# Attention, a gated feed-forward and a routed layer of eight experts: pairs of halves between the whole slots, splits issued further ahead

## The chip, the cores and the metric

The kernel runs on one core of a Trainium2 chip. The metric is the device time of one execution in microseconds. Three runs of the kernel before gave 978.3, 983.58 and 983.2, median 983.2. The engines are TensorE (PE; PEld is its weight load), VectorE (DVE), ScalarE (ACT), GpSimd (POOL) and SyncE (SP), which issues most of the transfers. Each works through its own queue in program order.

## The reference, cut to what matters

```python
scores = cap * np.tanh(scale * q @ k.T / cap)     # 4 batches, 12 heads, 448 x 64
x = softmax(scores) @ v                           # -> 1792 tokens x 768
x = (silu(x @ w_gate) * (x @ w_val)) @ w_out      # 768 -> 1536 -> 768
do_compute = x @ w_skip > 0                       # other tokens pass unchanged
e = argmax(x @ w_route, axis=1)                   # one of 8 experts per token
out = x + softmax(x @ w_route)[e] * (relu(x @ w1[e]) @ w2[e])   # 768 -> 1024 -> 768
```

## The kernel before, in words

Up to about 747 us the kernel does attention and the feed-forward layer, four batches after one another. The change touches what follows: the expert layer. Tokens are sorted by expert into **slots** of 128 rows. A whole slot holds tokens of one expert. What is left over of two experts, at most 64 tokens each, shares a slot as a **pair of halves**. Program text is laid out for four whole slots (0 to 3; slots 0 and 1 are filled from the first three batches, before the last is routed) and two pairs, here called P0 and P1 (`NWHOLE`, `NPAIRS`, `FETCHED`). More slots stand behind conditions at the end, which these inputs don't meet.

A whole slot needs its expert's w1 and w2 as eight **pieces** of 128 x 1536 numbers (768 KB). In this text piece 2.5 is the sixth piece of slot 2. `first(i)` multiplies the slot's tokens by piece i (i = 0 to 3) into a half of the hidden layer, 9 matmuls of 512 columns; after every second one ScalarE applies relu (L1066). `turn_h` transposes a half of the hidden layer on TensorE, ScalarE casts it to rounded numbers rh and VectorE forms the rest rl; `second(i)` multiplies by piece 4 + i, 12 matmuls of 384 columns; `turn_x` transposes the next slot's tokens; `finish` (L1086) weighs the result, adds the tokens and scatters the rows.

A whole slot works in rounded parts: `split_next` (L1008) rounds a loaded piece on ScalarE (wh, L1014) and subtracts on VectorE (wl, L401), and three products stand for one. A piece of a pair stays whole (`parted` is False): a pair needs sixteen pieces, two experts' eight, P0.4a and P0.4b for its ninth and tenth, takes two of them per `first` or `second`, and multiplies them in full precision, half of the rows each, without a split.

What sets the order around the change:

- `so["raw"]`: the rooms that pieces are loaded into, eight in the expert layer: three of attention's rooms (two pair_room and head_room; here R0, R1 and H) and five opened late (raw0 to raw4; here w0 to w4).
- `so["pair"]`: the pairs of buffers for a split piece's two parts, seven: three from the pool "early" (gh0 and gl0 to gh2 and gl2), two in `more`, two in the r64 pool.
- `load_next` (L996) issues the next load on SP's queue if a room is free; `coming`, `todo`, `held` (loaded, not split) and `ready` (split, or whole) are lists kept while the program is written. `used` gives buffers back.
- `piece` (L1027), called by every `first` and `second`, issues loads while there are rooms, then, in the slots behind `LATE`, at most one split, as long as fewer than `AHEAD` (5) pieces are ready.
- `LATE` (L68) is an order written out by hand for what stands between the last feed-forward unit and slot 2: slots 0 and 1 with the last routing chain among them. `choose`, `count`, `ranks`, `tiles`, `experts`, `places`, `gates`, `at` and `entries` are short VectorE chains; `listed0` and `listed1` are matmuls that make the token lists, after which VectorE writes the index row (L1327); `gather` fetches a slot's tokens by it (L952, GpSimd); `halves0`, `halves1` and `hidden0`, `hidden1` are `turn_h`, `rows1` and `rows2` are `turn_x` of slots 1 and 2; `split` is `split_next`.
- Behind `LATE`, `slot` (L1096) runs slot 2, slot 3, P0 and P1, in this order:

```python
for i in range(4):
    first(i, n)
    if i == 2:
        turn_h(0, n=n)
second(0, n)
turn_h(1, n=n)
second(1, n)
if ahead is not None:
    turn_x(ahead)
second(2, n)
second(3, n)
finish(s)
```

Of the kernel before, what the change touches and what calls it, by code (L numbers as in the profile page):

```python
# [7 lines left out]
F32 = mybir.dt.float32  # L8
F32R = mybir.dt.float32r
# [15 lines left out]
NWHOLE = 4  # L25
NPAIRS = 2
FETCHED = 2
# [7 lines left out]
AHEAD = 5  # L35
# [30 lines left out]
    chain store  # L66
""".split()
LATE = """  # L68
    choose first1 count ranks first2 hidden0 lows0 tiles first3 experts second0 hidden1 lows1 split second1 places
    split second2 rows1 gates split second3 finish0 first0 at split first1 entries split first2 listed0 halves0 split  # L70
    first3 listed1 gather gather gather gather second0 halves1 split second1 rows2 split second2 split second3 finish1
""".split()


# [1 line left out]
def tile_attn_moe_moe(  # L76
# [26 lines left out]
    PIECE = 1536  # L103
    MAXWHOLE = FETCHED + (N + (E - 1) * 63 + 127) // 128
# [30 lines left out]
    count = const.tile([T, E], F32, name="count")  # L135
    fit = const.tile([T, 6, E], F32, name="fit")
    early = const.tile([T, FETCHED], F32, name="early")
# [23 lines left out]
    def scratch(room):  # L161
        used = [0]

        def take(*shape):
            n = 1
            for d in shape:
                n *= d
            a = room[:, used[0]:used[0] + n]
            used[0] += n
            assert used[0] <= room.shape[1]  # L170
            if len(shape) == 1:
                return a
            names = " ".join("abc"[:len(shape)])
            return a.rearrange(f"p ({names}) -> p {names}", **dict(zip("abc", shape)))

        return take
# [41 lines left out]
    def gates(b):  # L218
        gt, sh = gate[:, NC * b:NC * b + NC], rt["sh"]
        nc.scalar.activation(out=sh, in_=sh, func=ACTF.Exp)  # L220
        yield V.tensor_reduce(gt, sh, axis=AX.X, op=ALU.add)
        yield V.tensor_scalar(gt, gt, EPS, None, op0=ALU.add)
        yield V.reciprocal(gt, gt)
# [148 lines left out]
    def slot_pieces(e_reg):  # L372
        a = [
            (w1[bass.ds(e_reg, 1), 128 * kk:128 * (kk + 3), 512 * half:512 * half + 512], 3)
            for half in range(F2 // 512) for kk in range(0, KD, 3)
        ]
        return a + [(w2[bass.ds(e_reg, 1), 128 * f:128 * (f + 2)], 2) for f in range(0, KF2, 2)]

    def load_piece(raw, piece):
        src, n = piece  # L380
        nc.sync.dma_start(
            out=raw.rearrange("p (k f) -> p k f", k=n), in_=src.rearrange("o (k p) f -> p (o k) f", p=128)
        )
# [3 lines left out]
    def expert(src):  # L387
        return nc.values_load(src, engines=SP, min_val=0, max_val=E - 1)

    def pieces_of(s):  # L390

        if s < FETCHED:
            return [(p, True) for p in slot_pieces(expert(early_i[0:1, s:s + 1]))]
        if s < MAXWHOLE:
            return [(p, True) for p in slot_pieces(expert(es_i[0:1, s:s + 1]))]
        o = MAXWHOLE + 2 * (s - MAXWHOLE)
        both = zip(*(slot_pieces(expert(es_i[0:1, o + i:o + i + 1])) for i in range(2)))
        return [(p, False) for ps in both for p in ps]

    def split_low(engine, low, full, high):  # L400
        engine.tensor_tensor(low, full, high.bitcast(F32), op=ALU.subtract)  # L401
# [25 lines left out]
    def whole(exact):  # L427
        with ExitStack() as ph:

            def pools(side):  # L430
                stack = ph.enter_context(ExitStack())

                def pool(name, bufs, **kw):
                    kw.setdefault("reuse_waits", "tile")
                    return stack.enter_context(tc.tile_pool(name=name, bufs=bufs, side=side, **kw))

                return stack, pool
# [466 lines left out]
            so = {"raw": [], "pair": [], "xg": [], "auto": False}  # L904

            def open_early():
                qks[0][0].close()
                right.close()
                _, pool = pools("right")
                p = pool("early", 1)  # L910
                psum = pool("ps_e", 1, space=PSUM)
                so["raw"] += [x[:, 0:PIECE] for x in pair_room + [head_room]]
                so["pair"] += [[p.tile([128, PIECE], F32R, name=f"{n}{i}") for n in ("gh", "gl")] for i in range(3)]
                so["odd"] = p.tile([128, PIECE], F32R, name="gl3")
                so["xg"] += [p.tile([128, DM], F32, name=f"xg{i}") for i in range(FETCHED)]
                so["x"] = [p.tile([128, KD, 128], F32R, name=n) for n in ("xgh", "xgl")]
                so["h"] = [[p.tile([128, KF2 // 2, 128], F32R, name=f"{n}{i}") for n in ("rh", "rl")] for i in range(2)]
                so["room"] = p.tile([128, 1024], F32, name="big_room")[0:T]
                so["row"] = p.tile([128, S], F32, name="row2")
                so["ph"] = [psum.tile([128, 512], F32, name=f"ph{i}") for i in range(2)]  # L920
                so["tp"] = [psum.tile([128, 512], F32, name=f"tp{i}") for i in range(2)]
                for xg in so["xg"]:
                    nc.gpsimd.memset(xg, 0.0)
# [62 lines left out]
            def turn_h(half, later=None, n=1):  # L986
                src = so["hid"][:, 512 * half:512 * half + 512]
                if n == 1:
                    turned(*so["h"][half], src, later)
                else:  # L990
                    turned(so["h32"][:, KF2 // 2 * half:KF2 // 2 * (half + 1)], None, src)


            coming, todo, held, ready = [], [], [], []

            def load_next():  # L996
                while so["raw"] and not todo:
                    if not coming:
                        return False
                    todo.extend(pieces_of(coming.pop(0)))  # L1000
                if not so["raw"]:
                    return False
                piece_, parted = todo.pop(0)
                held.append((so["raw"].pop(0), parted))
                load_piece(held[-1][0], piece_)
                return True

            def split_next():  # L1008
                raw, parted = held.pop(0)
                if not parted:  # L1010
                    ready.append((raw,))
                    return
                wh, wl = parts = so["pair"].pop(0)
                nc.scalar.copy(wh, raw)  # L1014
                split_low(nc.vector, wl, raw, wh)
                so["raw"].append(raw)
                ready.append(parts)
# [9 lines left out]
            def piece():  # L1027
                while load_next():
                    pass

                n = 1
                while so["auto"] and held and len(ready) < AHEAD and (not held[0][1] or n and so["pair"]):
                    n -= held[0][1]
                    split_next()
                if not ready:
                    split_next()
                return ready.pop(0)
# [75 lines left out]
            at = {load_part: 8}  # L1113
# [149 lines left out]
            for word in OPENING:  # L1263
                name = word.rstrip("0123456789")
                x = int(word[len(name):])
# [36 lines left out]
            b, last, take = B - 1, so["last"], scratch(so["late"][0:T])  # L1302

            def all_of(*chains):
                return lambda: [any(False for _ in chain()) for chain in chains]
# [13 lines left out]
            def list_(b0):  # L1319
                for b in range(b0, b0 + 2):  # L1320
                    listed(pl, rhs_[b % 2], rt["rv"][:, NC * b:NC * b + NC], b == 0, b == B - 1)
                    if b < 2:
                        put(b + 2, rhs_[b])
                if b0:
                    to = lists[:, :, FETCHED:]
                    V.tensor_tensor(to, to, pl.rearrange("p (a s) -> p a s", a=2), op=ALU.add)
                    V.tensor_copy(idx[:, FETCHED:], to[:, 0])  # L1327
# [4 lines left out]
                while load_next():  # L1332
                    pass

            order = list(range(NWHOLE)) + [MAXWHOLE + i for i in range(NPAIRS)]
            gathered = iter(order[FETCHED:])

            def next_gathered():
# [5 lines left out]
            while load_next():  # L1344
# [4 lines left out]
                "places": all_of(lambda: places(rank, take)), "at": all_of(lambda: last_at(take, room)),  # L1349
                "entries": all_of(entered), "experts": all_of(experts_known),  # L1350
                "listed0": lambda: list_(0), "listed1": lambda: list_(2),
                "gates": all_of(lambda: gates(b)), "split": split_next,
                "hidden0": lambda: turn_h(0, 0), "hidden1": lambda: turn_h(1, 1),
                "lows0": lambda: split_low(V, *lows.pop(0)), "lows1": lambda: split_low(V, *lows.pop(1)),
                "gather": next_gathered, "finish0": lambda: finish(0), "finish1": lambda: finish(1),
# [28 lines left out]
    with tc.manual_schedule():  # L1384
# [57 lines left out]
        with tc.If(big > 0) as cmp:  # L1442
            whole(True)
        with cmp.Else():
            whole(False)
# [31 lines left out]
```

## Time and profile before

| | us |
|---|---|
| median of three runs | 983.2 |
| the profiled execution | 982.64 |
| its span | 980.9 |
| PE busy in the span | 898.1 (92%) |
| DVE busy | 580.1 (59%) |
| ACT busy | 465.1 (47%) |
| POOL busy | 99.1 (10%) |

Busy shares are means over stages with different limits; the expert layer is the last quarter of the span. Times in rows count from the start of the span. [...]

### The profile page before, as it was taken

What the parts mean: (1) busy time and instruction counts of PE and PEld (TensorE: products, weight loads), DVE (VectorE), ACT (ScalarE), POOL (GpSimd) and SP (SyncE); (2) the same over time, 40 slices, a digit from 0 to 9 for tenths busy, and PEclk for the clock granted to TensorE, in tenths of its full rate; (3) what the DMA queues carried; (4) which work ended last, traced back from release to release, by engine and by line L of the source; (5) the groups of instructions that cost most, each with busy time, mean ns of one, the idle gap of its engine ahead of it and who ended that gap; (6) DMA issues with size and microseconds to landing.
All of it is one profiled execution on the core that took longest, in us unless ns stands there. A gap on an engine that the chain in (4) does not pass through costs nothing. (4 is left out here: it accounts for less than half of the span.)

```text
span 980.9 us, 12535 instructions
## 1 busy us (share of the span) xinstructions
PE 898.1 (92%) x4664; PEld 676.4 (69%) x4664; DVE 580.1 (59%) x906; ACT 465.1 (47%) x553; POOL 99.1 (10%) x66
## 2 busy tenths in 40 slices
PE   6899999999999999999999999999999775665984
PEld 2236787776788888778888888999987663544521
DVE  2768899998377666557666743565664943332000
ACT  5887667656464556446555532333342341313100
POOL 1000000000022221212221220000101020000000
PEclk9999999999999999999999999999999988667998
DMA  6996888898764344257343235453376654332894
GB/s 134 195 262 177 221 240 233 227 256 214 185 154 110 84 125 125 57 115 178 94 110 106 65 84 130 134 198 125 90 223 194 211 174 164 108 131 96 310 391 159
DMA packets 226020, 161.55 MB, mean 165 GB/s; under 512 B 158860, under 2 KB 186508, under 8 KB 225936
## 3 DMA queue, kind: packets, MB, share of 16 engines
q1 hardware_dynamic: 224048, 157.12, 57.1%
q0 software_dynamic: 960, 3.16, 0.9%
q8 instruction: 43, 0.70, 0.3%
q14 instruction: 41, 0.34, 0.1%
q10 hardware_dynamic: 928, 0.23, 0.1%
HBM read 140.01 MB, written 22.02 MB: 165 GB/s over the span
## 5 line engine op out<-in xcount | busy, mean ns | idle before, releaser
L748 PE MATMUL mo<-xhl,wh 128*128 128x448 f32 x576 | 215.1, 373 | 0.0
L750 PE MATMUL mo<-xhl,wl 128*128 128x448 f32 x576 | 210.4, 365 | 0.0
L749 PE MATMUL mo<-xhl,wh 128*128 128x448 f32 x576 | 210.3, 365 | 0.0
L401 DVE TENSOR_TENSOR wl<-raw,wh 128x768 fp32r<-128x768 f32 x108 | 117.1, 1084 | 69.8 <-ACT wh L735 69.0
L735 ACT CAST wh<-raw 128x768 fp32r<-128x768 f32 x108 | 89.9, 833 | 76.5 <-PE mo L749 49.5
L748 PEld LDWEIGHTS mo<-xhl,wh 128*128 128x128 f32 x576 | 108.1, 188 | 22.2 <-issue 11.0
L750 PEld LDWEIGHTS mo<-xhl,wl 128*128 128x128 f32 x576 | 108.2, 188 | 8.9 <-DVE wl L401 0.2
L749 PEld LDWEIGHTS mo<-xhl,wh 128*128 128x128 f32 x576 | 108.3, 188 | 7.9
L748 PE MATMUL mo<-hh,wh 128*128 128x448 f32 x288 | 108.2, 376 | 1.1 <-ACT x L795 1.1
L750 PE MATMUL mo<-hh,wl 128*128 128x448 f32 x288 | 105.3, 366 | 0.0
L749 PE MATMUL mo<-hl,wh 128*128 128x448 f32 x288 | 105.3, 366 | 0.0
L787 ACT ACTIVATE s<-mo 128x448 f32<-128x448 f32 x48 | 26.1, 544 | 110.6 <-PE mo L750 107.7
L535 ACT ACTIVATE arena<-ps,inv_sb 112x896 f32<-112x896 f32 x72 | 68.8, 1008 | 4.9 <-PE ps L525 4.9
L542 ACT ACTIVATE arena<-arena,cap_sb 112x1792 f32<-112x1792 f32 x36 | 64.6, 1793 | 1.1
L748 PEld LDWEIGHTS mo<-hh,wh 128*128 128x128 f32 x288 | 54.1, 188 | 11.8 <-issue 4.9
L570 POOL TENSOR_TENSOR sums<-arena 112x896 f32<-112x896 f32 x11 | 23.2, 2111 | 385.7 <-ACT arena L542 385.7
L750 PEld LDWEIGHTS mo<-hh,wl 128*128 128x128 f32 x288 | 54.1, 188 | 4.6
L749 PEld LDWEIGHTS mo<-hl,wh 128*128 128x128 f32 x288 | 54.1, 188 | 4.1
L581 PE MATMUL bank<-arena,arena 112*64 112x448 f32 x264 | 54.9, 548 | 1.3 <-ACT w L706 0.8
L790 DVE SCALAR_TENSOR_TENSOR s<-s,mo 128x448 f32<-128x448 f32 x48 | 29.6, 616 | 32.4 <-PE mo L750 31.5
L706 ACT ACTIVATE w<-raw 128x768 f32<-128x768 f32 x36 | 32.9, 914 | 31.3 <-DVE wl L401 13.6
L1086 DVE SCALAR_TENSOR_TENSOR o<-py,lists,xg 128x768 f32<-128x768 f32 x6 | 6.1, 1017 | 69.3 <-PE py L1050 69.3
(283 smaller groups left out, 1368.6 us busy)
## 6 DMA issues: line engine op xcount, KB each, us to landing
raw<-ws SPq DMA_DIRECT2D x54, 768.0 KB, 4.7
raw<-in_moe_w_dram SPq DMA_DIRECT2D x35, 768.0 KB, 6.4
pair_room<-in_moe_w_dram SPq DMA_DIRECT2D x20, 768.0 KB, 6.0
ws<-w SPq DMA_DIRECT2D x36, 384.0 KB, 5.8
raw<-in_moe_w_gate_dram SPq DMA_DIRECT2D x12, 768.0 KB, 5.9
raw<-in_moe_w_val_dram SPq DMA_DIRECT2D x12, 768.0 KB, 5.5
raw<-in_moe_w_out_dram SPq DMA_DIRECT2D x12, 768.0 KB, 5.1
head_room<-in_moe_w_dram SPq DMA_DIRECT2D x9, 768.0 KB, 5.9
```

Source lines behind the costliest of these rows:

```text
L401: engine.tensor_tensor(low, full, high.bitcast(F32), op=ALU.subtract)
L535: nc.scalar.activation(out=t[:, j], in_=ps[:, :, 0:S], func=ACTF.Tanh, scale=inv_sb[0:T])
L542: nc.scalar.activation(out=ts[part], in_=ts[part], func=ACTF.Exp, scale=cap_sb[0:T])
L570: nc.gpsimd.tensor_tensor(sm, ts[0][:, 0], ts[0][:, 1], op=ALU.add)
L581: nc.tensor.matmul(pv[64 * i:64 * i + 64], lhsT=hd["vn"][:, i, c], rhs=hd["t"][c // 2][:, c % 2, i], start=c == 0, stop=c == NC - 1,)
L706: nc.scalar.activation(out=w32, in_=raws[u][:, :, 1].bitcast(F32), func=ACTF.Abs)
L735: nc.scalar.copy(wh, w32s[w])
L748: nc.tensor.matmul(ps, lhsT=wh, rhs=mh, start=start, stop=False)
L749: nc.tensor.matmul(ps, lhsT=wh, rhs=ml, start=False, stop=False)
L750: nc.tensor.matmul(ps, lhsT=wl, rhs=mh, start=False, stop=stop)
L787: nc.scalar.activation(out=s, in_=cur[op], func=ACTF.Tanh, scale=0.5)
L790: nc.vector.scalar_tensor_tensor(s, in0=s, scalar=0.5, in1=cur.pop(op), op0=ALU.mult, op1=ALU.mult)
```

## The change

The slots now run in the order 0, 1, 2, P0, 3, P1. `piece` may issue two splits per call instead of one, and only split pieces count against `AHEAD`. `LATE` has more `split` words (sixteen where nine were, and their place moves: the chains places, gates, at and entries and the lists stand behind more of them); such a word does nothing if no piece is held or no pair is free. When a piece that stays whole is to be loaded, no room is free and no piece that has to be split is held, `load_next` takes one of the three early pairs that is free out of `so["pair"]` for good and adds its two buffers to `so["raw"]` as rooms. So the rooms become fourteen and the pairs four.

```diff
 LATE = """
-    choose first1 count ranks first2 hidden0 lows0 tiles first3 experts second0 hidden1 lows1 split second1 places
-    split second2 rows1 gates split second3 finish0 first0 at split first1 entries split first2 listed0 halves0 split
-    first3 listed1 gather gather gather gather second0 halves1 split second1 rows2 split second2 split second3 finish1
+    choose first1 count ranks first2 hidden0 lows0 tiles first3 experts second0 hidden1 lows1 split second1 split
+    split second2 rows1 split second3 finish0 split first0 places split gates split first1 at split first2 halves0
+    entries split split first3 split listed0 second0 halves1 split listed1 gather gather gather gather split second1
+    split rows2 split second2 split split second3 finish1 split
 """.split()
...
-                so["pair"] += [[p.tile([128, PIECE], F32R, name=f"{n}{i}") for n in ("gh", "gl")] for i in range(3)]
+                so["pair"] += [
+                    [p.tile([128, PIECE], F32R, tag=f"{n}{i}", name=f"{n}{i}") for n in ("gh", "gl")] for i in range(3)
+                ]
+
+                so["lent"], so["early"] = list(so["pair"]), p
...
             def load_next():
-                while so["raw"] and not todo:
+                if so["raw"] and not todo:
                     if not coming:
                         return False
                     todo.extend(pieces_of(coming.pop(0)))
+
+                if not so["raw"] and todo and not todo[0][1] and not any(x[1] for x in held):
+                    for i, parts in enumerate(so["lent"]):
+                        if any(parts is x for x in so["pair"]):
+                            so["pair"] = [x for x in so["pair"] if x is not parts]
+                            so["lent"][i] = None
+                            so["raw"] += [
+                                so["early"].tile([128, PIECE], F32, tag=f"{n}{i}", name=f"{n}{i}_whole") for n in ("gh", "gl")
+                            ]
+                            break
...
-                n = 1
-                while so["auto"] and held and len(ready) < AHEAD and (not held[0][1] or n and so["pair"]):
+                n = 2
+                while so["auto"] and held and (
+                    not held[0][1] or n and so["pair"] and sum(len(x) > 1 for x in ready) < AHEAD
+                ):
                     n -= held[0][1]
                     split_next()
...
+            def split_if():
+                while load_next():
+                    pass
+                if held and so["pair"]:
+                    split_next()
+
-            order = list(range(NWHOLE)) + [MAXWHOLE + i for i in range(NPAIRS)]
+            order = list(range(NWHOLE))
+            for i in range(NPAIRS):
+                order.insert(FETCHED + 1 + 2 * i, MAXWHOLE + i)
...
-                "gates": all_of(lambda: gates(b)), "split": split_next,
+                "gates": all_of(lambda: gates(b)), "split": split_if,
```

## Rows read from the trace of the kernel before

**Rows 1.** The page's strip of forty slices: TensorE's granted clock in tenths.
```profile
PEclk9999999999999999999999999999999988667998
```
**Rows 2.** Windows: stretch, length, PE, PEld, DVE, ACT, POOL busy, clock, DMA, GB/s.
```profile
811.00:861.00 50.00, 30.79 (x98) 24.70 (x98) 17.20 (x14) 14.18 (x14) 2.29 (x1) 0.73 0.41 135
861.00:913.00 52.00, 33.56 (x101) 26.27 (x103) 15.83 (x12) 11.53 (x12) 2.27 (x1) 0.67 0.38 128
913.00:937.00 24.00, 23.89 (x128) 9.28 (x124) 0.85 (x2) 3.23 (x6) 0.98 (x1) 1.00 0.89 335
937.00:971.00 34.00, 27.41 (x119) 9.63 (x118) 1.54 (x2) 2.37 (x4) 0.98 (x1) 1.00 0.87 329
```
**Rows 3.** TensorE's waits, 811 to 913: total us, times, longest; the largest.
```profile
PE py L1050 <- ACT gh L1014: 12.2, 6, 2.1
PE py L1050 <- DVE gl L401: 7.9, 6, 1.4
PE ph L1050 <- DVE gl L401: 7.4, 5, 2.5
...
```
**Rows 4.** Timeline of slot 2: start, us, engine; idle before and its releaser.
```profile
825.16 0.59 ACT L967 CAST rh<-tp 128x512 fp32r<-128x512 f32 x1 [6.01 <-PE tp L966]
825.64 1.48 ACT L1014 CAST gh<-raw 128x1536 fp32r<-128x1536 f32 x1
...
827.15 1.76 DVE L401 TENSOR_TENSOR gl<-raw,gh 128x1536 fp32r<-128x1536 f32 x1 [0.68 <-ACT gh L1014]
...
828.96 0.79 PE L1050 MATMUL ph<-gl,xgh 128*128 128x512 f32 x1 [1.29 <-DVE gl L401]
```
**Rows 5.** Windows in slot 3, TensorE's clock behind unbroken matmuls; columns as in rows 2.
```profile
866.00:869.00 3.00, 3.00 (x8) 2.32 (x8) 0.00 (x0) 0.00 (x0) 0.00 (x0) 0.50 0.99 372
869.00:872.00 3.00, 1.00 (x4) 0.43 (x3) 0.00 (x0) 1.96 (x2) 0.00 (x0) 0.97 0.49 189
```
**Rows 6.** Timeline of TensorE in slot 0: first2, the one wait, slot 1's start.
```profile
754.65 0.48 PE L1050 MATMUL ph<-gh,xgh 128*128 128x512 f32 x1
...
765.48 0.45 PE L1050 MATMUL py<-gh,rl 128*128 128x384 f32 x1 [1.00 <-DVE rl L401]
...
770.07 0.39 PE L1050 MATMUL ph<-gh,xgh 128*128 128x512 f32 x1
```
**Rows 7.** VectorE from low 0.7 to the index row: timeline, and one window.
```profile
765.36 1.74 DVE L401 TENSOR_TENSOR gl<-pair_room,gh 128x1536 fp32r<-128x1536 f32 x1
767.02 0.36 DVE L248 TENSOR_TENSOR late_room<-rank,steps 112x208 f32<-112x208 f32 x1
...
790.10 0.18 DVE L1327 CAST idx<-lists 128x22 uint32<-128x22 f32 x1
...
765.36:790.28 24.92, 19.50 (x103) 16.72 (x104) 22.64 (x44) 8.64 (x11) 1.03 (x1) 0.93 0.54 175
```
**Rows 8.** The gathers on GpSimd's queue: the first, and issue to landing of four.
```profile
791.08 1.04 POOL L952 DMA_INDIRECT xg<-out_dram,idx  x1 [16.07 <-DVE idx L1327]
...
DMA to landing us min/median/max: 4.0/5.8/7.5
```
**Rows 9.** Transfers: issue to landing of lone pieces in slot 2; P1's full window.
```profile
raw<-in_moe_w_dram SPq DMA_DIRECT2D x2, 768.0 KB, 4.3
...
939.00:954.00 15.00, 13.09 (x50) 4.10 (x46) 0.00 (x0) 1.78 (x3) 0.05 (x1) 1.00 1.04 391
```
**Rows 10.** Timeline: starts of slot 2, P0, its second0; P0's end; the last finish.
```profile
810.01 0.40 PE L1050 MATMUL ph<-gh,xgh 128*128 128x512 f32 x1
...
912.50 0.64 PE L1050 MATMUL ph<-head_room,late_room 128*64 128x512 f32 x1
...
923.59 0.49 PE L1050 MATMUL py<-head_room,late_room 128*64 128x384 f32 x1
...
936.25 0.49 PE L1050 MATMUL py<-pair_room,late_room 128*64 128x384 f32 x1
...
970.25 1.02 DVE L1086 SCALAR_TENSOR_TENSOR o<-py,lists,xg 128x768 f32<-128x768 f32 x1 [32.45 <-PE py L1050]
```

## The prediction, made before the changed kernel was run

> **What bounds the kernel now.** I read the strip of forty slices first: TensorE's granted clock stands at full speed until slice 32 and sinks only after it [rows 1]. So the windows by slot come next. Slots 2 and 3, the whole slots gathered late, take 50 and 52 us, with TensorE busy for 30.8 and 33.6 of them at a mean clock of 0.73 and 0.67, VectorE for 17.2 and 15.8, ScalarE for 14.2 and 11.5, and the DMA engines for about 0.4. None is full: a chain of waits. P0 (the first pair of halves) is another stage, TensorE busy for 23.9 of 24.0 us; P1 waits for its weights, with the DMA engines at 0.87, and at 1.04 in its first half [rows 2, 9].
>
> The waits of TensorE in slots 2 and 3 say which chain: first for the rounded part of a piece (ScalarE, L1014), then for its rest (VectorE, L401), in nearly every piece [rows 3]. The timeline shows why: ScalarE casts rh, which waits for TensorE's transposes, only then rounds the next piece, 1.48 us, then VectorE subtracts, 1.76 us, and TensorE starts in earnest 3.8 us after the cast began [rows 4]. In program order a split stands one piece ahead, on the wrong side of a cast or relu that waits for TensorE. [...]
>
> **The change, in program order.** I followed the lists raw, pair, held and ready through the new LATE and the slots, as the program is written. I name pieces by slot and number (2.5), a pair's by halves (P0.4a, P0.4b).
>
> *Slots 2 and 3.* At the start of slot 2 its pieces 2.0 to 2.6 are split; 2.7 follows in it. In slot 3 pieces 3.0 to 3.3 are split before it starts, the other four as each of the four pairs left comes free. What is then the limit? TensorE at full clock: in slot 0 it went from 754.65 to 770.07 through six of eight pieces and the three groups of transposes, 1.2 us of that a wait [rows 6]. With two more pieces at 2.1 us (nine matmuls at 0.23, the spacing there) a slot takes 14.2 + 4.2 = 18.4 us. VectorE has 17.2 and 15.8 us of work in these slots [rows 2], the eight subtractions of 1.66 among it [rows 7], and ScalarE less: hidden under TensorE, though VectorE barely. In slot 3 the tightest split, 3.4, can start after the first piece (2.1), takes 1.5 + 1.8, and is wanted after four pieces and a transpose (9): 3.6 us of slack. Both slots together went from 810.0 to 912.5 [rows 10], 102.5 us, and now take 36.8: **-65.7**. The bounds: 17.2 each, if VectorE's work alone counted, and 50 and 52, if nothing got ahead.
>
> *Slot 1 pays for it.* The six extra splits stand on VectorE ahead of the token lists. From low 0.7 to the index row took 24.9 us, 22.6 busy [rows 7]. Now: 22.6 + 6 x 1.66 + 0.6 (low half of halves1, now ahead) + 0.8 (low 2.2 waits for its rounding behind that cast) = 34.0, so the index is ready at 799.4 and not 790.3. TensorE is through first3 by 779 (770.1 and four pieces), stands at listed0 until the entries are there at 790, and again for the gather: issue 0.8 later, landing at least 4.0 us after that [rows 8], so 804.2. Then rows2 at half clock (1.1), second2 (12 matmuls of 384 columns at 1.2 GHz: 3.8) and second3 (2.1 to 3.8): 811 to 813, against 810.0. Taken: **+2.5**, for 812.5. Bounds: -4, if VectorE's small gaps go too and the clock holds; +9.1, if the whole delay is passed on.
>
> *P0 gets a new wait.* Slot 2 ends at 812.5 + 18.4 = 830.9. SP's queue, in order: P0.4a and b into the first lent pair, free when second1 of slot 2 ends (826.1); P0.5 a step later; P0.6 at 830.9; P0.7 after first0 of P0; 3.0 and 3.1 into w0 and w1 after first1. A piece lands 4.3 us after its issue on idle DMA engines [rows 9] and then one every 2.0 us (786 KB at 391 GB/s, [rows 9]). P0.4a lands at 830.4, the ninth and tenth, 3.0 and 3.1, at 846.4 and 848.4. ScalarE has them in its order right after relu0 of P0, and behind them stand the roundings of 3.2 and 3.3, which need the same two rooms again, and **behind those the cast h0 of P0**, which second0 needs. So: low 3.0 done 849.6, 3.2 issued and landed 853.9; low 3.1 done 851.6, 3.3 landed 855.9, rounded 857.4, cast 858.0. TensorE has done the four firsts of P0 by 842.0 (11.1 us, [rows 10]) and stands 16.0 us. Behind the wait are also relu1, all later matmuls of P0, and SP's 3.4 to P1, which are late by the same. After such a hole the clock is half [rows 5]: second0 takes 5.1 instead of 2.6. P0 goes from 24.1 to 42.5 us: **+18.4**, ending 873.4. Bounds: 0 (all hidden, as P0 shows now) and 23 (the two round trips of 4.3 to 7 us longer).
>
> [...]
>
> *P1.* Slot 3 ends at 873.4 + 18.4 = 891.8. Its pieces 3.4 to 3.7 and P1's follow each other from 861.4 at 2.0 us; the last two, into w4 and R1 after first0 of P1, land at 898.7 and 900.7, while second3 starts near 912. So P1 is no longer waiting for weights: 24.1 without its transposes for a follower (0.8), 23.4 us (33.6 before): **-10.2**. Last matmul at 915.2 instead of 970.2; the 10.65 us behind it, that begin with finish [rows 10], stay.
>
> *At nothing:* the lent rooms (an allocation, no instruction; their loads wait for matmuls that end anyway), the tags, `while` to `if`, counting only split pieces against AHEAD (the limit is met in slot 1 alone). Moving places and gates behind splits is in the VectorE sum; gathers in another order are four equal issues on POOL.
>
> **Sum.** The profiled execution took 982.64 (span 980.9 + 1.74). 2.5 - 65.7 + 18.4 - 10.2 = -55.0, so 927.6. The median, 983.2, is 0.6 above that execution: **928**. Within 917 to 939 if the mechanisms hold (the hole in P0 off by 6, slot 1 by 4).
>
> **Rivals.**
> - *The cast gets through* (ScalarE not held in P0: the four roundings find their data, because the lent rooms bring P0.4 to P0.6 in earlier). Then 16.0 + 2.5 fall away: 909. For: P0 shows no wait now. Against: 3.0 can't be issued before first1 of P0 gives w0 back, and 3.2 not before low 3.0.
> - *Slot 3 starves*: three of seven pairs are lent and never given back; with none spare, each split waits for a matmul. If slot 3 stays at 52 us, 33.6 of the gain are lost: 961. Against: the slack of 3.6 above.
> - *Nothing gets ahead, and it is slower.* If the splits still land behind the casts in slots 2 and 3 (50 and 52 us kept), the change leaves its prices, 2.5 + 18.4, less 10.2 in P1: 994. The point from which it decides: the two slots must give less than 10.7 us of the 65.7. Against: program order puts seven splits ahead of slot 2's first relu.
> - [...] The holes of 11, 4 and 16 us keep TensorE at half through the slots: 18.4 + 18.4 + 24.1 + 23.4 = 84 more, 1009 with the 2.5 counted already. It is slower once more than 55 of the 84 are lost. Against: [rows 5] shows full clock again behind one unbroken run of matmuls, and the slots have no hole of their own. [...]
>
> **Chances.** Forecast 0.72; cast gets through 0.11; slot 3 starves 0.10; nothing ahead 0.05; half clock 0.02. Everything but the last two is faster by over 0.5% (about what a measurement of this kernel tells from no change): 0.92, with 0.02 left for within 0.5%, and 0.06 slower. The range takes the forecast's own and the case below it, and part of the way to the starved slot: 905 to 947.
>
> **What would show it.** Right: finishes (L1086) of slots 2 and 3 follow the start of the slot by under 20 us, at a clock of 0.95 or more; the gathers start near 800; in P0 ScalarE idles before L1014 on a transfer, then a hole in TensorE of 13 to 19 us between first3 and second0; P1 without a wait for DMA. Wrong: L1050 waiting for L1014 or L401 in slots 2 or 3 by more than a few us, P0 without the hole, or rows2 waiting well past 806.

## The result and the profile after

The changed kernel takes 929.87 us (929.72 to 930.94, four runs), beside 980.76 for the kernel before in all its runs: a ratio of 0.9483 [0.9447, 0.9518]. The forecast was 928, in a range of 905 to 947.

The windows by slot of the changed kernel answer to [rows 2]; the columns are the same, and the clock is TensorE's granted clock as a share of full speed. The order is slot 2, P0, slot 3, P1.

```profile
814.90:833.30 18.40, 18.40 (x102) 16.55 (x102) 7.21 (x7) 6.09 (x8) 2.29 (x1) 1.00 0.67 219
833.30:877.50 44.20, 25.27 (x127) 9.61 (x127) 9.06 (x7) 8.91 (x10) 1.00 (x1) 0.77 0.85 311
877.50:895.90 18.40, 18.40 (x100) 16.55 (x102) 9.28 (x8) 8.82 (x10) 0.98 (x1) 1.00 1.04 393
895.90:918.20 22.30, 22.18 (x120) 8.48 (x119) 1.03 (x2) 2.36 (x4) 0.98 (x1) 1.00 0.43 161
```

The whole slots, 50 and 52 us before, take 18.4 each (18.3 and 18.4 from the first matmul of one slot to the first of the next, as the table below counts); TensorE is busy all the time and the clock is 1.00, not 0.73 and 0.67. P0 has become the slow one: 44.2 us with TensorE busy for 25.3. P1 is full where it waited before.

TensorE's waits in three stretches (764 to 800, 800 to 840 and 840 to 935; total us, times, longest) answer to [rows 3]:

```profile
PE last L266 <- DVE late_room L254: 10.0, 1, 10.0
PE py L1067 <- DVE rl L402: 1.0, 1, 1.0
...
PE tp L971 <- DMA xg<-out_dram,idx: 8.1, 1, 8.1
...
PE py L1067 <- ACT late_room L972: 18.9, 1, 18.9
```

No wait for the rounding or the subtraction of a piece is left. Three large holes are, all three foretold: the lists, the gather and the cast h0 of P0.

### The profile page after: what moved, and what is told of

It reads as the page before. It is cut to its first block, busy times and chain, and to the rows that moved or that the text cites. A ratio compares the mean times of both kernels' runs of the same rounds, so it can differ in the third digit from the quotient of the medians.

```text
span 928.0 us, 12526 instructions
## 1 busy us (share of the span) xinstructions
PE 865.9 (93%) x4664; PEld 659.0 (71%) x4664; DVE 578.9 (62%) x906; ACT 465.6 (50%) x553; POOL 99.2 (11%) x66
## 4 chain that ended last, share of the span: by engine, by line
PE 85%; DMA 4%; ACT 4%; DVE 4%; issue 2%; SPq 0%; POOL 0%; POOLq 0%; DVEq 0%; ACTq 0%
PE mo L749 20%; PE mo L751 19%; PE mo L750 19%; PE bank L582 7%; PE ps L526 7%; PE py L1067 5%; PE ph L1067 4%; DMA raw<-in_moe_w_dram 2%; PE mo L616 2%; DVE gl L402 2%; ACT arena L543 1%; ACT arena L536 1%; PE tp L971 1%; DMA xg<-out_dram,idx 1%; PE mo L819 1%
## 5 line engine op out<-in xcount | busy, mean ns | idle before, releaser
L571 POOL TENSOR_TENSOR sums<-arena 112x896 f32<-112x896 f32 x11 | 23.2, 2111 | 383.7 <-ACT arena L543 383.7
L526 PE MATMUL ps<-qkt 64*112 64x448 f32 x208 | 45.8, 559 | 0.0
```

The lines of the kernel that those rows point to most:

```text
L526: nc.tensor.matmul(ps[:, i, 0:S], lhsT=ks[rows_, 1, T * c:T * c + T], rhs=qs[rows_, 0], start=y == 0, stop=y == len(terms_) - 1,)
```

## What the stages came to

Times count from the start of the first subtraction behind experts (low 0.7), at 765.36 before and 763.50 after: the stages ahead, which the change leaves alone, came out 1.9 us shorter in this execution. Slot 2 began 44.65 us behind that mark and now begins 51.42 behind it, from 810.01 [rows 10] and 814.92.

| stage | forecast | measured |
|---|---|---|
| slot 1 | +2.5 | +6.8 |
| slots 2 and 3 (102.5 before) | -65.7 | -65.9 (36.6) |
| P0 (24.1 before) | +18.4 | +20.1 (44.2) |
| P1 (33.6 before) | -10.2 | -11.3 (22.3) |
| behind the last matmul (10.7 before) | 0 | -0.8 |
| ahead of the mark | 0 | -1.9 |
| span | -55.0 | -52.9 |

**The hole in P0.** ScalarE's timeline in P0 (start, us, then in brackets how long it idled and for what):

```profile
838.68 0.60 ACT L1083 ACTIVATE hid<-ph 128x512 f32<-128x512 f32 x1 [9.05 <-PE ph L1067]
850.85 1.47 ACT L1029 CAST more<-raw 128x1536 fp32r<-128x1536 f32 x1 [11.56 <-DMA raw<-in_moe_w_dram]
852.81 1.47 ACT L1029 CAST more<-raw 128x1536 fp32r<-128x1536 f32 x1 [0.50 <-DMA raw<-in_moe_w_dram]
858.62 1.47 ACT L1029 CAST gh<-raw 128x1536 fp32r<-128x1536 f32 x1 [4.34 <-DMA raw<-in_moe_w_dram]
861.35 1.47 ACT L1029 CAST gh<-raw 128x1536 fp32r<-128x1536 f32 x1 [1.26 <-DMA raw<-in_moe_w_dram]
862.73 0.58 ACT L972 COPY late_room<-tp 128x512 f32<-128x512 f32 x1
```

This is the order that was read from the program: relu0, then the roundings of 3.0 to 3.3, each waiting for its transfer, then the cast h0, for which TensorE stands. The forecast put it 27.1 us behind the start of P0 (858.0 less 830.9); it began 29.5 behind it. TensorE's timeline behind the hole shows the price of the clock:

```profile
863.36 0.90 PE L1067 MATMUL py<-gh_whole,late_room 128*64 128x384 f32 x1 [18.93 <-ACT late_room L972]
...
864.05 0.85 PE L1067 MATMUL py<-gh_whole,late_room 128*64 128x384 f32 x1
864.69 0.85 PE L1067 MATMUL py<-gh_whole,late_room 128*64 128x384 f32 x1
...
867.23 0.49 PE L1067 MATMUL py<-gh_whole,late_room 128*64 128x384 f32 x1
867.55 0.49 PE L1067 MATMUL py<-gh_whole,late_room 128*64 128x384 f32 x1
```

At first they start 0.64 us apart, in the end 0.32; the granted clock is 0.50 from 863.4 to 866.6 and 1.00 from 867.2 on. So second0 took 4.6 us, at half of the clock for most of it, where 5.1 was said and 2.6 is what it took before at a clock of 1.00 (from 923.59, with 0.32 us between the starts).

## The experiments

Each kernel is the changed one with one edit or two, timed beside the kernel before; a ratio is to the kernel before. The theory (A): the gain is the splits ahead; the hole in P0 is ScalarE's program order; the holes in slot 1 are VectorE's program order. The rival (B) gives the gain to the pair between the slots and to the lent rooms, and puts the holes down to the transfers or to the work that must be done anyway.

### The old order of the slots

```diff
-            order = list(range(NWHOLE))
-            for i in range(NPAIRS):
-                order.insert(FETCHED + 1 + 2 * i, MAXWHOLE + i)
+            order = list(range(NWHOLE)) + [MAXWHOLE + i for i in range(NPAIRS)]
```

> The changed kernel with the old order of the slots (0, 1, 2, 3, P0, P1); splits ahead and lent rooms stay. Theory A (the hole of 18.9 us in P0 comes from the place of four splits in ScalarE's program order, and the splits ahead bring the gain): no split is issued inside a pair any more, so P0 has no hole; P0.0a loads from about 827, 32 pieces at 2.0 us end near 893, P1 ends near 899 instead of 918, and the time is 911 (905 to 918). Theory B (the pair between the slots brings gain, because two pairs back to back wait for their weights): the hole goes, but P0 and P1 take some 33 us each again, 924 to 940.

914.6 us, ratio 0.9324 [0.9294, 0.9353]. Its windows of slot 2, slot 3, P0 and P1:

```profile
813.80:832.00 18.20, 18.20 (x100) 16.60 (x100) 13.39 (x11) 11.95 (x14) 2.29 (x1) 1.00 0.69 206
832.00:850.80 18.80, 18.80 (x104) 16.95 (x104) 10.97 (x9) 8.55 (x10) 2.26 (x1) 1.00 0.99 353
850.80:874.00 23.20, 23.20 (x129) 9.39 (x130) 1.02 (x1) 3.22 (x6) 0.98 (x1) 1.00 1.04 393
874.00:903.00 29.00, 25.61 (x122) 9.29 (x116) 1.19 (x2) 2.36 (x4) 0.98 (x1) 1.00 0.82 313
```

Within A's range (911 was expected), and against B: with the pairs back to back P0 doesn't wait at all, P1 takes 29 us instead of 22, and the hole of 18.9 is gone. With the splits where the change has them, the new order costs 15.3 us.

### No splits in a pair's slot before second2

```diff
-                    not held[0][1] or n and so["pair"] and sum(len(x) > 1 for x in ready) < AHEAD
+                    not held[0][1] or n and not so["hold"] and so["pair"] and sum(len(x) > 1 for x in ready) < AHEAD
...
                 n = 2 if s >= MAXWHOLE else 1
+                so["hold"] = n == 2
...
+                so["hold"] = False
                 second(2, n)
```

> The changed kernel, but a pair's slot issues no split before its second2; the four splits of slot 3 so stand behind the casts that P0 itself needs. Theory A: P0 24 to 25 us without a hole, slot 3 18.4, P1 bound by the last transfers (32 pieces from 828 at 2.0 us), last matmul near 897: 909 (904 to 914). Theory B (the hole is the transfers' own limit, the weights come no earlier whatever the order): the wait turns up again in slot 3 or P1, 924 to 932.

912.84 us, ratio 0.9302 [0.9279, 0.9324]. The windows of slot 2, P0, slot 3 and P1:

```profile
813.60:832.00 18.40, 18.40 (x102) 16.54 (x102) 7.18 (x6) 6.10 (x8) 2.29 (x1) 1.00 0.68 216
832.00:856.20 24.20, 24.20 (x131) 9.98 (x132) 6.39 (x6) 7.89 (x10) 1.00 (x1) 1.00 1.04 396
856.20:874.60 18.40, 18.40 (x101) 16.07 (x101) 12.59 (x10) 9.90 (x11) 2.24 (x1) 1.00 1.04 391
874.60:900.00 25.40, 23.05 (x116) 8.99 (x112) 0.20 (x1) 2.36 (x4) 0.98 (x1) 1.00 0.81 308
```

P0 is full. Its window reaches into slot 3: by TensorE's first matmuls (831.91, 855.11 and 873.47) P0 takes 23.2 us and slot 3 18.4. The same splits, moved behind the casts h0 and h1 and that of slot 3's tokens in ScalarE's queue, make no hole. Of the 21.0 us won in P0, P1 gives 3.9 back (26.3 us to the finish, for 22.4 by the same count): the DMA engines are now at 1.04 in P0 and slot 3. So the hole was the place in the queue (A); the transfers set the next limit (B's part in it).

### The old rule and the old LATE for splits

```diff
-                n = 2
-                while so["auto"] and held and (
-                    not held[0][1] or n and so["pair"] and sum(len(x) > 1 for x in ready) < AHEAD
-                ):
+                n = 1
+                while so["auto"] and held and len(ready) < AHEAD and (not held[0][1] or n and so["pair"]):
```

and `LATE` word for word as before.

> The changed kernel with the old LATE and the old rule of one split per piece; the new order and the lent rooms stay. Theory A: slot 1 as before (ends near 808), slot 2 50 us again, P0 without a hole because the splits of slot 3 stand one by one behind its casts, slot 3 paced by transfers at 2.0 us a piece, some 20 us, P1 23 to 26: 942 (934 to 955). Theory B, which is the prediction's slower rival (nothing gets ahead and the prices stay): 994, or 969 if slot 3 too is back at 50 us and only the hole is gone.

945.54 us, ratio 0.9632 [0.9607, 0.9656]; 942 was expected. The windows of slot 2, P0, slot 3 and P1:

```profile
813.00:863.00 50.00, 30.75 (x100) 24.60 (x98) 16.20 (x11) 11.43 (x12) 2.29 (x1) 0.73 0.43 140
863.00:892.50 29.50, 29.50 (x154) 14.05 (x153) 8.73 (x7) 10.03 (x11) 1.01 (x1) 1.00 1.03 395
892.50:907.20 14.70, 13.01 (x76) 11.55 (x76) 9.16 (x9) 7.86 (x10) 2.24 (x1) 1.00 1.04 391
907.20:935.00 27.80, 25.43 (x120) 9.00 (x118) 1.19 (x2) 2.37 (x4) 0.99 (x1) 1.00 0.80 302
```

Slot 2 is back at 50 us and a clock of 0.73. The second and third window are cut at finishes; by TensorE's first matmuls (863.16, 886.36 and 907.06) P0 takes 23.2 us and has no hole, and slot 3 takes 20.7 at full clock. Its splits come one per piece, behind the casts of P0, and the first five, from 883 to 892, each follow the landing of their piece. So with the lent rooms the new order does something even when the splits don't get ahead in slot 2; the order without the lent rooms was not run. The prediction's slower rival, 994, kept 52 us in slot 3 and 18.4 for a hole in P0, and neither is there: in these kernels a hole in P0 came only where splits stood ahead of a cast that P0 needs, and here none does.

One expectation failed: slot 1 was to end near 808, as before, and slot 2 starts at 813.0, 49.4 us behind the mark for 44.65. VectorE is as busy as before up to the index row (22.6 us), but TensorE's clock is lower, 0.76 for 0.93. More on this in the last section.

### No rooms lent

```diff
-                so["lent"], so["early"] = list(so["pair"]), p
+                so["lent"], so["early"] = [], p
```

> The changed kernel without lending: eight rooms, seven pairs throughout. Theory A: the rooms come free later, so 3.0 to 3.3 are loaded after second0 of P0 and their splits stand behind cast h1 and ahead of the cast of slot 3's tokens; the hole moves to the start of slot 3 and shrinks to 4 to 8 us: 918 (912 to 926). Theory B (the lent rooms feed the pairs): without them P0 and P1 wait for weights for 10 us more each, 935 to 950.

929.78 us, ratio 0.9476 [0.9452, 0.9499]: the same as the change, neither 918 nor 935. ScalarE from the cast h1 of P0 to the cast of slot 3's tokens, and then TensorE's longest wait:

```profile
847.67 0.58 ACT L972 COPY late_room<-tp 128x512 f32<-128x512 f32 x1 [2.48 <-PE tp L971]
856.58 1.47 ACT L1029 CAST more<-head_room 128x1536 fp32r<-128x1536 f32 x1 [8.32 <-DMA head_room<-in_moe_w_dram]
...
867.06 1.47 ACT L1029 CAST gh<-pair_room 128x1536 fp32r<-128x1536 f32 x1 [1.25 <-DMA pair_room<-in_moe_w_dram]
868.43 0.85 ACT L972 CAST xgh<-tp 128x384 fp32r<-128x384 f32 x2
...
PE ph L1067 <- ACT xgh L972: 11.6, 1, 11.6
```

The hole moved where A put it, behind cast h1 and ahead of slot 3's tokens, but it is 11.6 us and not 4 to 8: 3.0 was rounded only at 856.6, when it had landed. The hole is 7.3 us smaller than in the change. Slot 3 behind it takes 22.3 us instead of 18.4 (granted clock 0.57 in its first 6 us), and P1, with eight rooms, 25 for 22: nearly all of the 7.3 is used up. In this order lending is worth nothing that can be measured; the next kernel, beside the first, shows what it is worth in the other.

### Splits alone: old order, nothing lent

The two edits above together (old order, nothing lent).

> Only the splits of the change: new LATE and the new rule of splits per piece; the old order of the slots, nothing lent. Theory A (the splits ahead are all of the gain): slots 2 and 3 at 18.3 each, P0 starts near 851 with eight pieces in, the other 24 follow from 854 at 2.0 us each, P1 ends near 907 against 902 with lent rooms: 918 (913 to 925). Theory B (splits ahead gain only with pairs between the slots or with rooms lent): 935 or more.

921.39 us, ratio 0.9400 [0.9363, 0.9436]. TensorE's waits from 800 on:

```profile
PE tp L971 <- DMA xg<-out_dram,idx: 7.4, 1, 7.4
PE py L1067 <- SPq L1399: 2.1, 2, 1.1
PE py L1067 <- DMA pair_room<-in_moe_w_dram: 1.9, 2, 1.0
PE ph L1067 <- DMA raw<-in_moe_w_dram: 1.9, 2, 1.0
PE ph L1067 <- DMA pair_room<-in_moe_w_dram: 0.9, 1, 0.9
```

The splits by themselves are 0.9400, the whole change 0.9483. The seven short waits, 6.8 us, are for pieces of the pairs (the two put down to SP's queue stand in step with the others, two pieces of 2 us apart or a multiple of it). With lent rooms three of them are left, 3.1 us, and P0 and P1 together take 52.1 us instead of 58.1: that is what lending gives in the old order, 921.4 to 914.6, ratios 0.9400 and 0.9324.

### Lists ahead of the splits

```diff
-    choose first1 count ranks first2 hidden0 lows0 tiles first3 experts second0 hidden1 lows1 split second1 split
-    split second2 rows1 split second3 finish0 split first0 places split gates split first1 at split first2 halves0
-    entries split split first3 split listed0 second0 halves1 split listed1 gather gather gather gather split second1
-    split rows2 split second2 split split second3 finish1 split
+    choose first1 count ranks first2 hidden0 lows0 tiles first3 experts second0 hidden1 lows1 split second1 split split
+    second2 rows1 split second3 finish0 split first0 places gates first1 at first2 halves0 entries first3 listed0 split
+    listed1 gather gather gather gather split second0 halves1 split split second1 split split rows2 split split
+    second2 split split second3 finish1 split
```

> The changed kernel with LATE in another order: places, gates, at, entries, both lists and the gathers stand ahead of the splits from 1.5 on, and listed1 ahead of second0. Theory A (the two holes of TensorE in slot 1, 10.0 us at listed0 and 8.1 at the gather, come from the subtractions that stand ahead of the lists on VectorE): entries end near 783 instead of 788, the index is there near 789 instead of 800, slot 2 starts 10 to 11 us earlier: 919 (914 to 924). Theory B (VectorE has the same work to do before slot 2 whatever its order, so TensorE waits for pieces 1.4 to 1.7 instead): 927 to 932.

922.93 us, ratio 0.9414 [0.9378, 0.9451]; the interval just touches that of the change, [0.9447, 0.9518]. TensorE's waits from 760 to 835:

```profile
PE last L266 <- DVE late_room L254: 5.0, 1, 5.0
PE tp L971 <- DMA xg<-out_dram,idx: 2.1, 1, 2.1
PE py L1067 <- DVE rl L402: 1.9, 2, 1.3
```

10.0 and 8.1 became 5.0 and 2.1, so the place on VectorE's queue made half of the first and three quarters of the second (A); what is left of them has no experiment here. Slot 2 starts 39.9 us behind the mark instead of 51.4 (805.72 less 765.87), 11.5 earlier, but only 7 arrive in the median, and 8 behind the mark: slot 2 takes 19.9 instead of 18.4, now with more of the splits in it (VectorE busy for 12.8 us of it instead of 7.2), and the hole in P0 grows from 18.9 to 21.1.

### Lists first, with the hold, and with the old order

> Lists first and splits held in the pair's slot, together. Theory A: the two gains are in different stages and add up, and the transfers move with slot 2: 912.8 - 10.5 = 902 (897 to 908). Theory B (P1 is bound by transfers already, so an earlier slot 2 is given back there): 909 to 914.

906.51 us, ratio 0.9247 [0.9211, 0.9283].

> Lists first with the old order of the slots, lent rooms kept. Theory A: 914.6 - 10.5 = 904 (899 to 910). Theory B as for the kernel before it: 911 to 916.

906.58 us, ratio 0.9251 [0.9217, 0.9285]. Both beat the change by 23 us and lie in A's ranges, 4.5 and 2.6 us above the sums 902 and 904. In the first the difference is in the slots: slot 2 takes 19.8 us and slot 3 20.4, where the kernel with the hold alone had 18.3 and 18.4, and P1 27.1 for 26.3. In the second all four slots take what they took with the old order alone (P1 28.7 us for 29.0), but slot 2 starts only 8.4 us earlier behind the mark. The two can't be told apart in time: once the splits get ahead and no queue is blocked, it makes no difference here where the first pair stands.

## Why the prediction was right, point by point

- **What bounded the kernel** was read rightly: with the splits ahead the slots ran at 18.3 and 18.4 us and full clock, the sum from slot 0's rows. One term of that sum does not agree with its row: the wait taken off as 1.2 us is 1.00 there [rows 6], which gives 18.6. The windows by slot, of stages in which no engine was full, were the reading that decided.
- **P0's hole** was read from program order, in place and cause; the "hold" kernel shows the cause. It was 2.9 us longer: ten pieces took 24.4 us from the issue of P0.4a (828.43) to the landing of 3.1 (852.81), where 4.3 + 9 x 2.0 = 22.3 was said, and 3.3 had a round trip of 5.2 instead of 4.3.
- **Slot 1 was mis-sized**, +6.8 for +2.5. Three terms were off; the rows of the first two:

```profile
796.53 0.69 DVE L402 TENSOR_TENSOR rl<-tp,rh 128x512 fp32r<-128x512 f32 x1 [2.14 <-ACT rh L972]
...
799.81 0.18 DVE L1344 CAST idx<-lists 128x22 uint32<-128x22 f32 x1
...
807.87 1.54 PE L971 MATMUL tp<-ident,xg 128*128 128x128 f32 x6 [8.08 <-DMA xg<-out_dram,idx]
```

  - The index row was done 36.5 us behind the mark against 34.0 said. VectorE's work was right (33.0 us busy up to there, for 33.2); the sum had 0.8 us for its waiting, and it waited 2.14 us for rh alone, which TensorE's transposes, behind the hole at listed0, brought late.
  - From the index row to rows2 it took 7.9 us where 4.8 was said (0.8 + 4.0). I took 4.0 us [rows 8] for the gather that TensorE waits for. That row has the landing of two of the four gathers only, the third (4.0) and the fourth (7.5), and 5.8 is the mean of these two; of the first the trace has no landing. In the changed kernel the first took 7.0. Of that, 0.7 is its longer issue (last section); why the rest is longer than 4.0 no run isolates. So one sign of being wrong came in part: rows2 waited past 806, to 807.9.
  - Behind the gather the clock came back sooner than said, 7.1 us to slot 2 for 8.3: it was 0.50 from 807.8 to 812, 0.71 in the microsecond after and 1.00 from 813 on. No run shows the 1.2 GHz from which the 3.8 us of second2 were worked out, since the traces have the clock only as a share of full speed; second2 took 3.8 us (809.06 to 812.84), nearly all of it at 0.50, and second3 2.1.
- **P1** gained as said, by transfers during slot 3 (DMA share 1.04 there).
- **The rival "the cast gets through"** named the time (909) of a kernel that had only to hold its splits back (912.8). **"Slot 3 starves"** did not come: four pairs were enough. **"Half clock"** did not come either: 1.00 in both slots. The hole of 18.9 us in P0 was followed by 0.50, that of 11.6 with no rooms lent by a mean of 0.57 over 6 us; the waits of 1.0 to 1.1 us in P1 with the old order left a mean of 1.00.
- **In part it was luck.** The span came out 2.1 us longer than said, and this is what is left of larger misses that cancel: +4.3 in slot 1 and +1.7 in P0, against -1.1 in P1, -0.8 behind the last matmul and -1.9 ahead of the mark, where the change touches nothing. Beside the kernel before in all its runs (980.76) the gain is 50.9 us, where 55 was said.
- What the prediction did not ask is whether each part was worth having. The splits alone give 0.9400, lending takes that to 0.9324, and the order to 0.9483: one of the three parts cost 15 us of what the other two brought, as long as splits stand in the pair's slot. With these held back it costs nothing (0.9302). The gain of the splits is that of the new `LATE` and the new rule together; no run takes these apart.

The change's `LATE` has eighteen `split` words; the count of sixteen in the section on the change is wrong, while the working followed the diff itself.

## What to carry to other kernels

Work issued ahead is not free if its engine runs in program order: before a prefetch or a split moves up, list what stands behind it in that queue and when its data lands. Here four splits, put ahead of a cast that TensorE was to wait for, made a hole of 18.9 us, and moving them behind it brought 17 us. And test a change of several parts by its parts: a stage that looks like the point of the change (the pair between the slots) can be the one that loses.

## What the runs showed of the hardware that was not expected

**An indirect transfer's issue took longer beside VectorE's subtraction.** Two gathers and two scatters of the changed kernel, and VectorE beside three of them:

```profile
800.79 1.77 POOL L957 DMA_INDIRECT xg<-out_dram,idx  x1 [25.83 <-DVE idx L1344]
802.87 1.32 POOL L957 DMA_INDIRECT xg<-out_dram,idx  x1 [0.31 <-issue]
...
817.57 2.29 POOL L1108 DMA_INDIRECT out_dram<-o,idx  x1 [10.76 <-DVE o L1103]
...
897.17 0.98 POOL L1108 DMA_INDIRECT out_dram<-o,idx  x1 [17.35 <-DVE o L1103]
...
799.90 3.42 DVE L402 TENSOR_TENSOR gl<-raw,gh 128x1536 fp32r<-128x1536 f32 x2
...
817.20 1.75 DVE L402 TENSOR_TENSOR gl<-raw,gh 128x1536 fp32r<-128x1536 f32 x1
```

It took 0.98 us with VectorE idle, and 1.32, 1.77 and 2.29 beside a subtraction, 0.3 to 1.3 us more. The first gather of the kernel before, with VectorE idle, took 1.04 [rows 8]. The times look like those of a wait: the issue ends 0.9 us after the subtraction that it met, which is nearly its whole length alone. At 817.57 it ends at 819.86, the subtraction at 818.95; the second gather ends at 804.19, the subtraction at 803.32; the first ends at 802.56, between the two subtractions of its line, of which the earlier ends at 801.65. So the splits ahead delayed the gather twice: by standing ahead of the index row, and by 0.7 us in its issue. What links the issue and the subtraction no run shows.

**The same hole can cost more or less clock.** In slot 1 the kernel before and the one with the old rule and `LATE` have the same wait of 5.0 us for the same subtraction, and the same matmuls behind it. TensorE's granted clock is back at 1.00 from 784 on in the first, about 4 us behind the hole (it ends at 780.2). In the second it stays at 0.50 up to 790, some 12 us behind the hole (it ends at 778.4), and so the way from the mark to the index row takes 28.9 us instead of 24.9. The same two microseconds, before and with the old rule (the clock stands third from the end):

```profile
784.00:786.00 2.00, 2.00 (x20) 2.00 (x20) 1.50 (x3) 0.00 (x0) 0.00 (x0) 1.00 0.29 24
...
784.00:786.00 2.00, 2.00 (x11) 2.00 (x12) 0.98 (x2) 0.00 (x0) 0.00 (x0) 0.50 0.85 298
```

What made the difference no run shows.
